# Row loads, normalisation, transposes and late modulation rows rearranged in an adaLN linear-attention and SwiGLU block

## The chip, the cores and the metric

The kernel runs on one core of a Trainium2 chip. A core has five engines, each with its own in-order instruction queue: TensorE (PE, with weight loads shown as PEld), VectorE (DVE), ScalarE (ACT), GpSimd (POOL) and SyncE (SP, which only issues transfers here). SP, ACT and POOL can issue DMAs. The metric is device microseconds of one execution; the times below are medians over several executions, and the profile is of one more.

## The reference

`x` is 2048 rows of 1024 (bf16). A conditioning vector `c` gives six modulation rows of 1024 through `w_mod`. With `H = 32` heads of width 32:

```python
mod = (_silu(c) @ w_mod).reshape(c.shape[0], 6, 1, -1)
sa, ca, ga, sb, cb, gb = ...
h = _layernorm(x, axis=-1) * (1 + ca) + sa
x = x + ga * _A_ref(h, A_wqkv, A_wo)          # linear attention
h = _layernorm(x, axis=-1) * (1 + cb) + sb
x = x + gb * _B_ref(h, B_w_gate, B_w_up, B_w_down)   # SwiGLU, F = 3584
# in _A_ref: q, k, v = split(x @ wqkv); phi(t) = where(t > 0, t + 1, exp(t)) + 1e-6
kv = einsum('bhsd,bhse->bhde', phi(k), v); z = einsum('bhsd->bhd', phi(k))
o = (phi(q) @ kv) / (phi(q) @ z + 1e-6); return o @ wo
```

## The kernel before

The 2048 rows are worked in four chunks of 512 (`sc` 0 to 3), each of four tiles of 128 rows (`st` 0 to 15; four a chunk). `M4` holds the normalised, transposed and modulated rows of a chunk as the matmul operand: 8 column blocks (`cc`) of 128 by 512.

The program is a list of labelled pieces of TensorE work in a hand-written order (`seq`), and a table of extra steps run after a piece (`put(label, step)`); nothing is reordered by a scheduler. The order is: the start with K of chunk 0, then V0 (eight groups), KV0 first half, Q0 first group, KV0 second half, the rest of Q0, K1, V1, KV1 first half, K2 first group, KV1 second half, the rest of K2, V2, and the same for K3 and V3, then Q1 to Q3 interleaved with the attention output, and the SwiGLU stage, which the change does not touch. Each group of K, V or Q is eight matmuls of 128x512 into one PSUM bank. `nextbank` hands out banks 0 to 4 in turn; a group that gets a bank must wait until its last user was read. Banks 5 to 7 hold the KV sums from KV0 on. K and Q groups are evacuated by `phi_to`: an exponential on ACT, then two operations on DVE. V groups are evacuated by one copy on ACT.

What the change touches:

- **Loads.** All loads go through the SP queue in program order: `c`, the row tiles (`load_x`, into six slots `xs`), the modulation weights of `ca` and `sa` in four steps (`load_wme`), K weights (`load_wk`), and V and Q weights (`load_cols`). Before, two row tiles come ahead of the first modulation step and two behind it.
- **Start.** `ln_a` takes mean and variance of a tile on DVE and `rstd` on POOL, `ln_nmr` the bias on DVE, `ln_xn_act` normalises on ACT. The four tiles of chunk 0 are transposed on TensorE (`tr0`) and copied to `M4` (`tr0_evac`, ACT for even tiles, DVE for odd). `mod_mm(p)` is 32 one-column matmuls into bank 7 that give two column blocks of `ca` and `sa`; `mod_apply(p)` copies them out and modulates these two blocks for all 512 rows. First K runs over the blocks for seven groups at once in banks 0 to 6, with `mod_mm(p + 1)` behind the tenth matmul of a step. `warm(n)` issues n matmuls on zeros.
- **Chunks 1 to 3.** `put_ln` places, two pieces apart, the statistics of a tile and the normalisation of the one before it (`ln_b`, on DVE), followed by `dma_start_transpose` on the ACT queue into `M4`. Then `modulate`, eight column blocks on DVE, in two steps.
- **Late modulation rows.** `ga`, `sb`, `cb`, `gb` (`LATE`): eight half rows, each loaded (`load_late`, 1 MB, three buffers) and multiplied (`late_mm`, 32 one-column matmuls), the two halves of a row into a bank from `nextbank` that is copied to `m1` by DVE after the second. `late_fin` makes `sbT`, `cb1T` or the spread copy `rep`; `late_bc` broadcasts `ga` or `gb` over the partitions by eight matmuls on `rep`. The multiplication of `wo` by `ga` is on DVE, in V2.

In the profile all buffers named `M...` show as `M`, PSUM banks as `bank`, and a line is that of the helper: L205 statistics, L211 `rstd`, L217 `nmr`, L223 and L228 normalise, L231 the transpose by DMA, L235 modulate, L248 to L250 `phi_to`, L253 K, L268 V, L276 Q, L285 KV, L316 and L319 a late piece and its copy, L327 `rep`, L334 broadcast, L341 transposes on TensorE, L379 `mod_mm`, L508, L514 and L533 the SwiGLU stage. L478 is the normalisation of the second layernorm, on POOL, L465 the attention output.

Of the kernel before, what the change touches and what calls it, by code (L numbers as in the profile page):

```python
# [21 lines left out]
def kernel(  # L22
# [13 lines left out]
    nc = tc.nc  # L36
# [114 lines left out]
    load_x(0)  # L151
    load_x(1)
    load_wme(0)
    load_x(2)
    load_x(3)
# [17 lines left out]
    mask = const.tile([P, KVW], BF16, name="mask")  # L173
    nc.gpsimd.memset(mask[:], 0.0)
    for j in range(HPC):
        rs = slice(j * DH, (j + 1) * DH)
        nc.gpsimd.memset(mask[rs, j * DH:(j + 1) * DH], 1.0)
        nc.gpsimd.memset(mask[rs, P + j:P + j + 1], 1.0)
    nc.gpsimd.memset(v_c[:, :, :, P:VW], 1.0)
# [21 lines left out]
    def ln_a(st):  # L201
# [10 lines left out]
        stat[st] = (mv, rstd)  # L212

    def ln_nmr(st):
        mv, rstd = stat[st]
# [5 lines left out]
    def ln_xn_act(st):  # L221
        rstd, nmr = stat.pop(st)
        nc.scalar.activation(out=xns[st % 6], in_=xs[st % 6], func=ACT.Identity, scale=rstd[:], bias=nmr[:])  # L223

    def ln_b(st):
        ln_nmr(st)
        rstd, nmr = stat.pop(st)
        nc.vector.tensor_scalar(out=xns[st % 6], in0=xs[st % 6], scalar1=rstd[:], scalar2=nmr[:],  # L228
                                op0=ALU.mult, op1=ALU.add)
        sc_, t = divmod(st, STC)  # L230
        nc.scalar.dma_start_transpose(out=M4[:, sc_, :, t * P:(t + 1) * P], in_=xns[st % 6])  # L231

    def modulate(sc_, cc, sT, c1T):
        h = M4[:, sc_, cc, :]
# [71 lines left out]
    late_acc = {}  # L306

    def late_mm(i):
        q, kb = LATE[i // 2][0], i % 2
        if kb == 0:  # L310
            late_acc[q] = nextbank()
        mps = late_acc[q]
        for ii in range(NB // P):
            col = kb * (NB // P) + ii
            for j in range(DC):
                nc.tensor.matmul(mps[:, col:col + 1], lhsT=wml[i % 3][:, j, ii * P:(ii + 1) * P],  # L316
                                 rhs=scT[:, j:j + 1], start=(j == 0), stop=(j == DC - 1))
# [32 lines left out]

    warm(14)
    ln_a(0)
    ln_a(1)
    ln_nmr(0)
    ln_xn_act(0)
    tr0(0)
    warm(2)
    ln_a(2)
    ln_nmr(1)
    ln_xn_act(1)  # L360
    tr0_evac(0)
    tr0(1)
    warm(2)
    ln_a(3)
    ln_nmr(2)
    ln_xn_act(2)
    tr0_evac(1)
    tr0(2)
    ln_nmr(3)
    ln_xn_act(3)  # L370

# [10 lines left out]
    def mod_apply(p):  # L382
# [5 lines left out]
        modulate(0, 2 * p, saT, ca1T)  # L388
# [304 lines left out]
```

## Time and profile before

| what | us |
|---|---|
| runs | 878.88, 883.75, 884.09 (median 883.75) |
| the profiled execution, whole | 880.06 |
| its span, first to last instruction | 878.3 |
| TensorE matmuls busy | 843.1 (96%) |
| VectorE busy | 331.5 (38%) |
| ScalarE busy | 144.1 (16%) |
| GpSimd busy | 58.9 (7%) |
| chain that ended last, TensorE's share | 88% |

The mean granted TensorE clock is 0.983. The three largest TensorE groups, L508, L514 and L533, are the SwiGLU stage, which begins near 249 us. A busy TensorE is not TensorE at its peak: a matmul of 512 columns counts as busy for 0.38 us on average while the next one already runs in its shadow, so prices are taken from the distance between starts. An idle time in the timeline stands in brackets behind the instruction that ends it, with the engine, tile and line whose end released it; where that engine had long been done, the release was another's.

### The profile page before, as it was taken

Reading aid. Unit: us, or ns where it says so; the run is one execution under the profiler, and the core shown is the slowest. Engines: PE = TensorE matmul, PEld = TensorE weight load, DVE = VectorE, ACT = ScalarE, POOL = GpSimd, SP = SyncE. Lnnn points to the kernel's source line nnn. Section 1 sums busy time; section 2 is a strip of 40 time slices with the busy share of each in tenths; the row PEclk is TensorE's granted clock in tenths of the full one; section 3 lists DMA queues with packets and bytes.
Section 4 is the critical chain, followed back from the end, with each engine's and each line's share of the span. In section 5 each row is a group of like instructions: output and inputs, shape, how many; then the busy total and the mean of one; then the engine's idle time right before and its main releaser. Section 6 shows DMA issues by size and latency. Waiting matters only on the chain.

```text
span 878.3 us, 10840 instructions
## 1 busy us (share of the span) xinstructions
PE 843.1 (96%) x4361; PEld 399.2 (45%) x4446; DVE 331.5 (38%) x643; ACT 144.1 (16%) x270; POOL 58.9 (7%) x114
## 2 busy tenths in 40 slices
PE   6989788899999999999999999999999999999998
PEld 3444343454444444444444444444444444444444
DVE  4557336629775565532121122121121221212212
ACT  4222222233231111111111000111100111100000
POOL 1010001001403222210000000000000000000000
PEclk6999889999999999999999999999999999999999
DMA  9984743404649889987788313555512455302220
GB/s 280 349 186 138 166 129 79 112 1 85 171 100 217 225 219 220 209 186 241 216 252 273 109 48 109 148 161 154 159 44 72 136 159 155 108 6 73 66 72 25
DMA packets 203764, 128.65 MB, mean 146 GB/s; under 512 B 50497, under 2 KB 189889, under 8 KB 203713
## 3 DMA queue, kind: packets, MB, share of 16 engines
q1 hardware_dynamic: 150336, 95.44, 37.2%
q10 hardware_dynamic: 51072, 24.12, 13.8%
q0 software_dynamic: 2304, 8.39, 2.5%
q8 instruction: 35, 0.57, 0.3%
q14 instruction: 17, 0.13, 0.1%
HBM read 103.81 MB, written 12.58 MB: 133 GB/s over the span
## 4 chain that ended last, share of the span: by engine, by line
PE 88%; DVE 5%; DMA 3%; issue 1%; ACTq 1%; ACT 1%; SPq 0%; POOL 0%; DVEq 0%
PE bank L514 22%; PE bank L533 22%; PE bank L508 22%; PE bank L465 6%; PE bank L276 6%; PE bank L253 5%; PE bank L268 2%; DMA M<-M 2%; DVE stats L205 1%; DVE M L250 1%; ACTq L231 1%; PE bank L438 1%; DMA M<-in_A_x_dram 1%; DVE e L249 1%; PE bank L285 1%
## 5 line engine op out<-in xcount | busy, mean ns | idle before, releaser
L514 PE MATMUL bank<-M,M 128*128 128x512 bf16 x881 | 210.4, 379 | 0.8
L508 PE MATMUL bank<-M,M 128*128 128x512 bf16 x871 | 209.7, 379 | 1.3
L516 DVE TENSOR_TENSOR M<-bank,e 128x512 bf16<-128x512 f32 x112 | 77.5, 692 | 275.1 <-PE bank L514 265.7
L533 PE MATMUL bank<-M,M 128*128 128x512 bf16 (+1 forms) x687 | 146.9, 370 | 0.6
L511 ACT ACTIVATE e<-bank 128x512 f32<-128x512 f32 x112 | 66.8, 597 | 439.7 <-PE bank L508 403.1
L533 PEld LDWEIGHTS <-M 128*128 128x128 bf16 x924 | 90.4, 98 | 103.3
L514 PEld LDWEIGHTS <-M 128*128 128x128 bf16 x896 | 87.7, 98 | 105.7
L508 PEld LDWEIGHTS <-M 128*128 128x128 bf16 x896 | 87.3, 98 | 103.9
L537 DVE TENSOR_TENSOR M<-bank,gb_bc 128x512 f32<-128x512 f32 (+1 forms) x33 | 22.3, 675 | 149.2 <-PE bank L533 135.3
L253 PE MATMUL bank<-M,M 128*128 128x512 bf16 x246 | 61.6, 396 | 9.8 <-DVE M L235 7.3
L268 PE MATMUL bank<-M,M 128*128 128x512 bf16 x247 | 58.1, 389 | 8.5 <-DVE m L319 5.2
L465 PE MATMUL bank<-M,M 128*128 128x512 bf16 x254 | 57.8, 379 | 0.1
L248 ACT ACTIVATE e<-bank 128x512 f32<-128x512 f32 x64 | 37.5, 598 | 118.5 <-PE bank L253 56.2
L276 PE MATMUL bank<-M,M 128*128 128x512 bf16 x250 | 56.6, 379 | 0.3
L533 PE MATMUL bank<-M 128*128 128x512 bf16 x219 | 50.7, 379 | 0.3
L249 DVE TENSOR_SCALAR e<-e 128x512 f32<-128x512 f32 x64 | 27.9, 436 | 50.5 <-ACT e L248 50.5
L250 DVE SCALAR_TENSOR_TENSOR M<-bank,e 128x512 bf16<-128x512 f32 x64 | 44.3, 692 | 3.6
L253 PEld LDWEIGHTS <-M 128*128 128x128 bf16 x256 | 24.7, 100 | 40.8 <-DVE M L235 12.5
L268 PEld LDWEIGHTS <-M 128*128 128x128 bf16 x256 | 25.3, 100 | 39.3 <-issue 11.6
L465 PEld LDWEIGHTS <-M 128*128 128x128 bf16 x256 | 24.9, 98 | 29.8
L276 PEld LDWEIGHTS <-M 128*128 128x128 bf16 x256 | 24.6, 98 | 27.9
L467 DVE TENSOR_TENSOR M<-bank,M 128x512 f32<-128x512 f32 x32 | 22.1, 690 | 14.4 <-PE bank L465 14.3
(66 smaller groups left out, 328.5 us busy)
## 6 DMA issues: line engine op xcount, KB each, us to landing
M<-in_B_w_gate_dram SPq DMA_DIRECT2D x56, 512.0 KB, 3.9
M<-in_B_w_up_dram SPq DMA_DIRECT2D x56, 512.0 KB, 5.1
M<-in_w_mod_dram SPq DMA_DIRECT2D x8, 1024.0 KB, 7.5
x_scratch<-M POOLq DMA_DIRECT2D x16, 512.0 KB, 5.8
M<-x_scratch ACTq DMA_DIRECT2D x16, 512.0 KB, 3.5
M<-in_B_w_down_dram SPq DMA_DIRECT2D x6, 1024.0 KB, 8.4
M<-in_A_x_dram SPq DMA_DIRECT2D x16, 256.0 KB, 7.6
M<-in_w_mod_dram SPq DMA_DIRECT2D x8, 512.0 KB, 7.0
```

The source lines that it names most:

```text
L248: nc.scalar.activation(out=e[:], in_=acc, func=ACT.Exp)
L249: nc.vector.tensor_scalar(out=e[:], in0=e[:], scalar1=1.0, scalar2=PHI_EPS, op0=ALU.min, op1=ALU.add)
L250: nc.vector.scalar_tensor_tensor(out=dst, in0=acc, scalar=0.0, in1=e[:], op0=ALU.max, op1=ALU.add)
L253: nc.tensor.matmul(acc[:], lhsT=M4[:, sc_, cc, t * P:(t + 1) * P], rhs=wk[:, cc, h * NB:(h + 1) * NB], start=(cc == 0), stop=(cc == DC - 1))
L268: nc.tensor.matmul(acc[:], lhsT=M4[:, sc_, cc, t * P:(t + 1) * P], rhs=wv[:, cc, h * NB:(h + 1) * NB], start=(cc == 0), stop=(cc == DC - 1))
L276: nc.tensor.matmul(acc[:], lhsT=wq[:, cc, qc * P:(qc + 1) * P], rhs=M4[:, sc_, cc, :], start=(cc == 0), stop=(cc == DC - 1))
L465: nc.tensor.matmul(acc[:], lhsT=oTs[st % 3][:, cc, :], rhs=wo[:, cc, hs], start=(cc == 0), stop=(cc == DC - 1))
L508: nc.tensor.matmul(g_ps[:], lhsT=wg_blk[:, cc, fs], rhs=M4[:, sc_, cc, :], start=(cc == 0), stop=(cc == DC - 1))
L511: nc.scalar.activation(out=sg[:], in_=g_ps[:], func=ACT.Silu)
L514: nc.tensor.matmul(u_ps[:], lhsT=wu_blk[:, cc, fs], rhs=M4[:, sc_, cc, :], start=(cc == 0), stop=(cc == DC - 1))
L516: nc.vector.tensor_tensor(out=gus[sc_][:, f, :], in0=u_ps[:], in1=sg[:], op=ALU.mult)
L533: nc.tensor.matmul(y_ps[:, 0:w], lhsT=gus[sc_][:, f, t * P:(t + 1) * P], rhs=wd(f)[:, c0:c1], start=(f == 0), stop=(f == FC - 1))
```

## The change

1. The four row tiles of chunk 0 are loaded ahead of the first modulation weights.
2. At the start the statistics of all four tiles come first; `nmr` moves from DVE to POOL; tile 2 is normalised on POOL, the other three on ACT; the masks and the ones of `v_c` are written on POOL behind that. First K begins tile by tile: the first two column blocks of tiles 0 and 1 are modulated and multiplied, then those of tiles 2 and 3, with the transposes of tile 3 and `mod_mm(1)` in between. Warm matmuls go from 14 + 2 + 2 to 21 + 3.
3. In chunks 1 to 3 `ln` takes statistics on DVE, `rstd`, `nmr` and the normalisation on POOL, and the transpose is issued on the SP queue. The labels are a little earlier.
4. The late rows accumulate in a free part of bank 7 (columns 320 and up), not in a bank from `nextbank`, and are spread over chunks 1 and 2 instead of chunk 1. The steps that use them, the load of `wo` and its multiplication by `ga` move back accordingly.

```diff
-    load_x(0)
-    load_x(1)
+    for st in range(STC):
+        load_x(st)
     load_wme(0)
-    load_x(2)
-    load_x(3)
     load_wk(0, 2)
...
         nmr = small.tile([P, 1], F32, name="nmr")
-        nc.vector.tensor_scalar(out=nmr[:], in0=mv[:, 0:1], scalar1=rstd[:], scalar2=-1.0,
+        nc.gpsimd.tensor_scalar(out=nmr[:], in0=mv[:, 0:1], scalar1=rstd[:], scalar2=-1.0,
                                 op0=ALU.mult, op1=ALU.mult)
...
+    def ln_xn(st, pool):
+        rstd, nmr = stat.pop(st)
+        if pool:
+            nc.gpsimd.tensor_scalar(out=xns[st % 6], in0=xs[st % 6], scalar1=rstd[:], scalar2=nmr[:],
+                                    op0=ALU.mult, op1=ALU.add)
+        else:
+            nc.scalar.activation(out=xns[st % 6], in_=xs[st % 6], func=ACT.Identity, scale=rstd[:], bias=nmr[:])
+
+    def ln(st):
+        ln_stats(st)
+        ln_xn(st, True)
         sc_, t = divmod(st, STC)
-        nc.scalar.dma_start_transpose(out=M4[:, sc_, :, t * P:(t + 1) * P], in_=xns[st % 6])
+        nc.sync.dma_start_transpose(out=M4[:, sc_, :, t * P:(t + 1) * P], in_=xns[st % 6])
...
-        if kb == 0:
-            late_acc[q] = nextbank()
-        mps = late_acc[q]
+        mps = bank[7][:, 320 + 8 * q:328 + 8 * q]
...
-                                 rhs=scT[:, j:j + 1], start=(j == 0), stop=(j == DC - 1))
+                                 rhs=scT[:, j:j + 1], start=False, stop=(j == DC - 1), skip_group_check=True)
...
+    warm(21)
+    for st in range(STC):
+        ln_stats(st)
+    ln_xn(2, True)
...
+    ln_xn(0, False)
+    tr0(0)
+    warm(3)
+    ln_xn(1, False)
+    tr0(1)
+    tr0_evac(0)
+    tr0_evac(1)
+    mod_mm(0)
+    mod_rows(0)
+    modulate(0, 0, saT, ca1T, 0, 2 * P)
+    modulate(0, 1, saT, ca1T, 0, 2 * P)
+    tr0(2)
+    ln_xn(3, False)
...
+    for g in (0, 1):
+        for cc in (0, 1):
+            kmm(bank[g], 0, G[g][0], G[g][1], cc)
     tr0(3)
     tr0_evac(3)
-    mod_apply(0)
...
+    for g in (2, 3):
+        for cc in (0, 1):
+            kmm(bank[g], 0, G[g][0], G[g][1], cc)
+    mod_mm(1)
+    mod_rows(1)
+    for g in (4, 5, 6):
+        for cc in (0, 1):
+            kmm(bank[g], 0, G[g][0], G[g][1], cc)
+    modulate(0, 2, saT, ca1T)
+    modulate(0, 3, saT, ca1T)
+    for p in (1, 2):
...
+    put_ln(1, [("V", 0, 1), ("V", 0, 2), ("V", 0, 3), ("V", 0, 4), ("Q", 0, 2), ("Q", 0, 3)])
     for sc in (2, 3):
...
+        put_ln(sc, [("K", sc - 1, 1), ("K", sc - 1, 3), ("K", sc - 1, 5), ("K", sc - 1, 7),
+                    ("V", sc - 1, 4), ("V", sc - 1, 6)])
-    put(("V", 0, 2), lambda: load_late(0), lambda: load_late(1), lambda: load_late(2))
+    put(("V", 0, 6), lambda: load_late(0), lambda: load_late(1), lambda: load_late(2))
...
-    lab = [("K", 1, i) for i in range(8)] + [("V", 1, i) for i in range(8)]
+    lab = [(k, sc, i) for sc in (1, 2) for k in ("K", "V") for i in (2, 6)]
...
+    put(("K", 1, 7), lambda: late_fin(2))
+    put(("V", 1, 1), lambda: late_bc(2, ga_bc))
+    put(("V", 1, 7), lambda: late_fin(3))
+    put(("K", 2, 0), lambda: nc.sync.dma_start(out=wo, in_=wo_v))
+    put(("K", 2, 7), lambda: late_fin(4))
+    put(("V", 2, 7), lambda: late_fin(5))
+    put(("K", 3, 1), lambda: late_bc(5, gb_bc))
     for cc in range(DC):
-        put(("V", 2, cc), lambda cc=cc: nc.vector.tensor_tensor(out=wo[:, cc, :], in0=wo[:, cc, :], in1=ga_bc[:],
+        put(("V", 3, cc), lambda cc=cc: nc.vector.tensor_tensor(out=wo[:, cc, :], in0=wo[:, cc, :], in1=ga_bc[:],
```

Three places show what moves. The lines of the changed kernel have other numbers. On ACT in V0 (CAST is the copy of a V group into `v_c`), before and now:

```order
L271 CAST M_81<-bank_73 128x4x128
L231 DMA_TRANSPOSE M_80<-M_83 128x8x128
L271 CAST M_81<-bank_74 128x4x128
L231 DMA_TRANSPOSE M_80<-M_83 128x8x128
L271 CAST M_81<-bank_70 128x4x128
```

```order
L260 CAST M_81<-bank_73 128x4x128
L260 CAST M_81<-bank_74 128x4x128
L260 CAST M_81<-bank_70 128x4x128
L260 CAST M_81<-bank_71 128x4x128
L260 CAST M_81<-bank_72 128x4x128
L237 ACTIVATE e<-bank_73 128x512
```

The transposes that stood between the copies are gone from ACT; the exponential of Q0 follows the last copy.

On DVE at the copy of a late row (`m`) and its spread copy `rep`, before in the middle of K1 and now at its end:

```order
L319 CAST m_131<-bank_73 128x8
L249 TENSOR_SCALAR e<-e 128x512
L250 SCALAR_TENSOR_TENSOR M_81<-bank_71,e 128x512
L205 BN_STATS stats<-M_83 128x6 x2
L207 BN_AGGR mv<-stats 128x2
L209 TENSOR_SCALAR veps<-mv 128x1
L217 TENSOR_SCALAR nmr<-mv,rstd 128x1
L228 TENSOR_SCALAR M_83<-M_83,rstd,nmr 128x1024
L327 COPY rep<-m_131 128x1024
```

```order
L304 CAST m_120<-bank_77 128x8
L238 TENSOR_SCALAR e<-e 128x512
L239 SCALAR_TENSOR_TENSOR M_81<-bank_73,e 128x512
L196 BN_STATS stats<-M_83 128x6 x2
L198 BN_AGGR mv<-stats 128x2
L200 TENSOR_SCALAR veps<-mv 128x1
L312 COPY rep<-m_120 128x1024
L224 TENSOR_SCALAR M_80<-M_80,ca1T,saT 128x512 x8
```

`nmr` and the normalisation have left DVE, the row is copied out of bank 7 instead of bank 3, and all eight modulations of chunk 2 follow `rep` directly.

On SP from the last weights of Q on, before and now:

```order
L148 DMA M_78<-in_A_wqkv_dram 128x8x512 x3
L304 DMA M_79<-in_w_mod_dram 128x8x512 x3
L137 DMA M_83<-in_A_x_dram 128x1024 x4
L304 DMA M_79<-in_w_mod_dram 128x8x512 x5
L607 DMA M_82<-in_A_wo_dram 128x8x1024
```

```order
L148 DMA M_78<-in_A_wqkv_dram 128x8x512 x3
L220 DMA_TRANSPOSE M_80<-M_83 128x8x128 x4
L293 DMA M_79<-in_w_mod_dram 128x8x512 x3
L137 DMA M_83<-in_A_x_dram 128x1024 x4
L220 DMA_TRANSPOSE M_80<-M_83 128x8x128
L293 DMA M_79<-in_w_mod_dram 128x8x512
L220 DMA_TRANSPOSE M_80<-M_83 128x8x128 x2
```

The four transposes of chunk 1 now stand between the weights of Q and the first late rows, and those of chunk 2 alternate with late loads.

More of the change, by code (lines that the diff above doesn't have):

```diff
@@ L172 @@
     nc.gpsimd.memset(den_eps_t[:], DEN_EPS)
[L173 to L179, printed above, removed]
     saT = const.tile([P, DC], BF16, name="saT")
@@ L590 @@
[L590 removed]
+        for t in range(STC):
+            put(labels[t], lambda t=t: ln(sc_ * STC + t))
+        for i in range(2):
+            put(labels[STC + i],
+                lambda i=i: [modulate(sc_, cc, saT, ca1T) for cc in range(4 * i, 4 * i + 4)])
+    put_ln(1, [("V", 0, 1), ("V", 0, 2), ("V", 0, 3), ("V", 0, 4), ("Q", 0, 2), ("Q", 0, 3)])
     for sc in (2, 3):
[L592 to L593 removed]
```

83 lines of the change are left out of this document (19 added, 64 removed).

## The prediction

> **What bounds the kernel now.** I read the page first (span, memory rate), then the TensorE timeline of the first 190 us, row by row, then what ACT, DVE and GpSimd do in each gap of it, then the landing times of transfers. The page:
>
> ```profile
> span 878.3 us, 10840 instructions
> ...
> GB/s 280 349 186 138 166 129 79 112 1 85 171 100 217 225 219 220 209 186 241 216 252 273 109 48 109 148 161 154 159 44 72 136 159 155 108 6 73 66 72 25
> ```
>
> A slice is 22 us. Transfers fill the first two (280 and 349 GB/s) and have room from then on. The change stands in the phases K, V and Q of the four row chunks, so the TensorE timeline there carries the rest (start us, duration, line, count, and in brackets the idle time ahead of it and who ended it):
>
> ```profile
> 16.83 1.01 PE L341 MATMUL bank<-ident,M 128*128 128x128 bf16 x8
> 19.43 0.61 PE L253 MATMUL bank<-M,M 128*128 128x512 bf16 x1 [1.58 <-DVE M L235]
> ...
> 31.84 6.08 PE L253 MATMUL bank<-M,M 128*128 128x512 bf16 x25
> 37.75 13.98 PE L268 MATMUL bank<-M,M 128*128 128x512 bf16 x63
> 51.56 1.07 PE L285 MATMUL bank<-M 128*128 128x129 bf16 x16
> 52.47 1.89 PE L276 MATMUL bank<-M,M 128*128 128x512 bf16 x8
> 54.20 0.28 PE L285 MATMUL bank<-M 128*128 128x129 bf16 x2
> ...
> 58.77 12.03 PE L276 MATMUL bank<-M,M 128*128 128x512 bf16 x54
> 70.64 3.62 PE L253 MATMUL bank<-M,M 128*128 128x512 bf16 x16
> 74.09 0.94 PE L316 MATMUL bank<-scT,M 128*128 128x1 bf16 x32
> 74.89 3.61 PE L253 MATMUL bank<-M,M 128*128 128x512 bf16 x15
> ...
> 88.35 1.89 PE L253 MATMUL bank<-M,M 128*128 128x512 bf16 x8 [1.89 <-DVE M L250]
> ...
> 96.22 0.59 PE L268 MATMUL bank<-M,M 128*128 128x512 bf16 x1 [5.20 <-DVE m L319]
> 97.02 5.05 PE L268 MATMUL bank<-M,M 128*128 128x512 bf16 x14 [0.22 <-issue]
> ...
> 115.48 1.07 PE L285 MATMUL bank<-M 128*128 128x129 bf16 x16
> 119.53 0.61 PE L253 MATMUL bank<-M,M 128*128 128x512 bf16 x1 [2.98 <-DVE M L235]
> ...
> 124.65 3.64 PE L253 MATMUL bank<-M,M 128*128 128x512 bf16 x16
> 128.13 0.61 PE L334 MATMUL bank<-ident,rep 128*128 128x128 bf16 x8
> ...
> 137.21 7.07 PE L268 MATMUL bank<-M,M 128*128 128x512 bf16 x31
> 146.28 3.61 PE L268 MATMUL bank<-M,M 128*128 128x512 bf16 x16 [2.01 <-DVE M L250]
> ...
> 154.03 1.07 PE L285 MATMUL bank<-M 128*128 128x129 bf16 x16
> 157.06 1.36 PE L253 MATMUL bank<-M,M 128*128 128x512 bf16 x4 [1.97 <-DVE M L235]
> ...
> 162.32 12.25 PE L253 MATMUL bank<-M,M 128*128 128x512 bf16 x55
> ```
>
> The undisturbed prices stand in it. V of chunk 0 is eight groups of eight matmuls from 37.75 to 51.56: 13.81, so 1.73 a group and 0.216 a matmul. Half of a KV step is 52.47 - 51.56 = 0.91. A piece of a late row (32 one-column matmuls) is 74.89 - 74.09 = 0.80. A broadcast is at most 0.61. TensorE is the bound: what it does not spend on these prices is what a schedule can win. From the end of Q0 on:
> - KV0's second half takes 54.20 to 58.77 = 4.57, due 0.91: 3.7 lost.
> - K1 and V1 with eight late pieces and one broadcast take 70.64 to 115.48 = 44.84, due 16 x 1.73 + 8 x 0.80 + 0.6 = 34.7: 10.1 lost. The brackets name it: a bank not yet evacuated (1.89), then 5.20 for the cast `m1` of a late row whose bank `nextbank` wants back.
> - KV1 with K2's first group, 115.48 to 124.65 = 9.17, due 2 x 0.91 + 1.73 = 3.55: 5.6 lost, begun by the wait for modulation (2.98).
> - V2, 137.21 to 154.03 = 16.82, due 13.81: 3.0 lost, begun by a late evacuation (2.01).
> - KV2 with K3's first group, 154.03 to 162.32 = 8.29, due 3.55: 4.7 lost, again modulation (1.97).
> Together 27.1. Part of it is no idle time but matmuls at a slow clock behind a gap (14 in 5.05 at 97.02, 0.36 each).
>
> **The start.** First K now begins at 19.43 and V0 at 37.75.
>
> ```profile
> 4.10 1.28 DVE L205 BATCH_NORM_STATS2 stats<-M 128x6 f32<-128x512 bf16 x2 [2.98 <-DMA M<-in_A_x_dram]
> ...
> 5.74 1.28 DVE L205 BATCH_NORM_STATS2 stats<-M 128x6 f32<-128x512 bf16 x2
> 5.91 0.56 POOL L211 TENSOR_TENSOR rstd<-veps,neg_half 128x1 f32<-128x1 f32 x1 [3.38 <-DVE veps L209]
> ...
> 9.89 1.29 DVE L205 BATCH_NORM_STATS2 stats<-M 128x6 f32<-128x512 bf16 x2 [2.32 <-DMA M<-in_A_x_dram]
> ```
> ```profile
> L476 POOL TENSOR_SCALAR nmr<-mv,rstd 128x1 f32<-128x1 f32 x16 | 4.8, 301 | 1.7
> ```
> ```profile
> 223.28 1.20 POOL L478 TENSOR_SCALAR M<-M,rstd,nmr 128x1024 bf16<-128x1024 f32 x1
> ```
>
> DVE needs 5.74 - 4.10 = 1.64 a tile and waits 2.32 for the third, which comes behind the first modulation weights. With all four tiles first, 1 MB is in at about the end of the second statistics, so DVE goes through: 4.10 + 4 x 1.64 = 10.7. Then GpSimd, in order: `rstd` 0.56, `nmr` 0.30 (now on GpSimd; the row is of the same form), normalising tile 2 at 1.20 (the nearest row has the same size with an f32 input): 12.7, with hand-overs 13.0. Eight transposes (1.01): TensorE starts first K at 14.0. The masks on GpSimd stand behind that and nothing needs them before KV0. The modulation weights of the first step come 0.5 MB later in the queue than before but, at 280 GB/s, 2.1 MB is in by 10, ahead of its use near 11.
>
> From 14.0 to V0: 64 matmuls at 0.216 = 13.8, three modulation pieces of 0.80 = 2.4, the last transposes 1.0, and some 1.2 for four hand-overs to DVE: 32.4. Saved 37.75 - 32.4 = 5.3. Cover: first K eats 1 MB of rows, 4.2 MB of modulation and 2.1 MB of K weights, 7.3 MB in all; the page's rates give 6.2 MB at 22 and the rest near 25.5, with about 1 us to complete 26.5; the last chunk is used near 27.6. So this cover is thin: 1 us. V weights and rows 4 to 7 follow the same queue and are wanted 5 us later than they land.
>
> **Transposes from ACT to SyncE.** In V0 the ACT queue now holds:
>
> ```profile
> 49.14 3.20 ACTq L231 DMA_TRANSPOSE M<-M  x1
> ...
> 52.46 3.28 ACTq L231 DMA_TRANSPOSE M<-M  x1
> ```
>
> ACT spends that time on issuing, and the copies of V behind it release KV0 late. On SyncE, twelve issues cost ACT nothing; KV0's 3.7 goes whole. What is queued behind a waiting transpose on SyncE: late weights, rows of the next chunk and `wo`. Chunk 1: DVE is done with K0's evacuations at about 42.7 - 5.3 = 37.4, GpSimd needs 0.56 + 0.30 + 1.20 with gaps 2.2 a tile, so tile 7 goes out at 37.4 + 1.64 + 4 x 2.2 = 47.8. Three late loads and four tiles behind it, 4.2 MB, are in near 62 at 349 GB/s with issue and completion; K1 begins at 32.4 + 13.8 + 2 x 0.91 + 13.8 = 61.8 and wants tile 8 two groups later at 65.3. Covered by 3.
>
> How long a transpose takes in SyncE's queue no row shows; on ACT's:
>
> ```profile
> DMA to landing us min/median/max: 3.0/5.2/14.2
> ```
>
> The 14.2 is the one beside `wo`; in one queue it follows the load instead of sharing with it, and `wo` now starts a chunk later. Deadlines from issue to landing: 11 us in chunk 1, about 8 in chunks 2 and 3 (tile 15 goes out near 24.5 after K2's start, the eight modulations must end at 32.7, they take 2.8, less overlap). I take 5.2, so the 5.6 and 4.7 go; I put back 0.5 for chunk 3. Ends: 0 and 9 for one chunk.
>
> **Normalise on GpSimd; late rows in bank 7.** DVE loses 0.55 + 0.20 and its waits for GpSimd per tile; late rows take no `nextbank` bank, so the 5.20 and 1.89 lose their cause. The pieces are the same eight; four move from K1/V1 to K2/V2, no change in the sum. What is late next is the broadcast of `ga`:
>
> ```profile
> 85.10 0.68 DVE L327 COPY rep<-m 128x1024 bf16<-128x1024 bf16 x1
> ```
> ```profile
> L248 ACT ACTIVATE e<-bank 128x512 f32<-128x512 f32 x64 | 37.5, 598 | 118.5 <-PE bank L253 56.2
> ...
> L250 DVE SCALAR_TENSOR_TENSOR M<-bank,e 128x512 bf16<-128x512 f32 x64 | 44.3, 692 | 3.6
> ```
> ```profile
> 222.35 0.43 DVE L249 TENSOR_SCALAR e<-e 128x512 f32<-128x512 f32 x1 [0.69 <-ACT e L248]
> ...
> 224.08 0.68 DVE L249 TENSOR_SCALAR e<-e 128x512 f32<-128x512 f32 x1 [0.57 <-ACT e L248]
> ```
>
> K1 ends on TensorE after 8 x 1.73 + 2 x 0.80 = 15.4, and the broadcast is due two groups later, at 18.9. DVE: exponential 0.60 + 0.2, then 0.43 + 0.69, statistics 1.64, `rep` 0.68: 15.4 + 4.3 = 19.7. TensorE waits 0.8. That is the low end. DVE's total in K1 is 8 x 1.12 + 4 x 1.64 = 15.5 against TensorE's 15.4, so it has no reserve, and GpSimd takes some: the L249 that began at 224.08, inside the normalise of 223.28 to 224.48, ended 0.28 after it and took 0.68 where the other took 0.43. An L249 that began with a normalise would wait 1.2. One in K1 caught early and one in part moves `rep` by 2: 2.8. I take 2. The Trainium skill (SBUF — State Buffer, Who interferes with whom) says that a DVE operation in a two-port mode and a GpSimd operation exclude each other for the whole instruction; the 0.68 row agrees, and by the page the whole 1.2 could be met at each normalise, which is the first rival.
>
> The multiplication of `wo` by `ga` moves to V3, where DVE has only that: hidden, eight at 0.68 in 13.8. It frees V2's evacuations, so the 3.0 goes.
>
> **Sum.** 5.3 + 27.1 = 32.4 off; 2.0 for `rep` and 0.5 for chunk 3 back: 29.9. The profiled execution took 880.06 for its span of 878.3, so 850.2 for one like it. The median of the runs shown, 883.75, is 3.7 above it and the lowest 1.2 below; I add 0.8 and say 851.
>
> **Rivals.**
> 1. GpSimd holds DVE in full: 0.56 + 0.30 + 1.20 = 2.1 at each of four tiles, 8.3 a chunk. Five banks give four groups less an evacuation, 6.9 - 1.9 = 5.0, so K itself waits some 3; `rep` would come 8 late, and tile 15 with it. 8 + 6 beyond what I have put back: 864. For it: the 0.68 row. Against: that row lost 0.25, and only L249 of the evacuations shows it.
> 2. Transposes land late: at 14.2 each, modulation misses K2's and K3's start by 3 and 6, each with a slow clock behind it (8 matmuls at 0.15 more, and half a KV step; 2.6), and K1's by 0 to 3. 15 back: 865. For it: SyncE's loads lie ahead of them. Against: the median.
> 3. First K runs slow: TensorE has gaps of 1 to 1.4 before 14.0. Its first 14 matmuls at 0.36 instead of 0.216 cost 2.0: 853, inside my range. Against: full speed behind the gaps at 88.35 (eight in 1.89). The Trainium skill (TensorE: Matmul & The Clock Gate, Part 1) has the clock fall after an idle window of about 3.4 us; the 2.98 gap with a slow clock behind it is shorter than that, the 5.20 one agrees.
> 4. Slower: the late rows wait for their weights. TensorE takes its instructions in order, and a late load stands behind waiting transposes on SyncE. Load i+3 is asked for behind piece i and used three pieces, twelve groups or 20.7 us, later; a transpose may hold it for the 5 us between two tiles. That leaves 16 for a load whose landing was
>
> ```profile
> DMA to landing us min/median/max: 5.5/7.5/11.7
> ```
>
> From 16 us on each further microsecond counts eight times; at 21 the gain is gone: (21 - 16) x 8 = 40 back, 890. Nothing shows such landings.
> 5. It does nothing: the gaps come back elsewhere, within 1% of before.
>
> **Chances.** My case 0.55 (846 to 857), first rival 0.17, second 0.12, third 0.08, slower 0.03, no effect 0.05. The range 845 to 865 takes in the first three rivals and leaves out the last two, and outliers of the others, 0.2 at most. A change of less than 1% (875 to 892) can't be told from none here. Faster 0.92, same 0.05, slower 0.03.
>
> **What would show it.** First K at 14 and V0 at 32 to 33, else the start is wrong. No idle time in KV0's second half. The broadcast of `ga` with a bracket of 0.8 to 2.8 naming `rep`. K2 and K3 beginning straight behind the half KV step: a bracket that names modulation, ended by a transpose, is the second rival. L249 with a mean near 0.45 is my case, above 0.8 the first rival. I'd be wrong altogether if V0 or K1 waited for tiles or weights: then SyncE's order is the new bound.

## The result and the profile after

The changed kernel takes 848.59 us (848.46 to 848.69), the kernel before, run beside it on the same chip, 881.32 (878.72 to 884.09): a ratio of 0.9628, interval 0.9588 to 0.9668. The predicted time was 851. From the page of the changed kernel, the span, the busy times, the transfer rate by slices and the chain that ended last:

```profile
span 846.8 us, 10977 instructions
...
PE 837.2 (99%) x4452; PEld 395.3 (47%) x4452; DVE 323.5 (38%) x617; ACT 143.9 (17%) x269; POOL 80.3 (9%) x143
...
GB/s 283 314 244 115 284 187 67 1 119 158 98 217 217 217 219 210 192 245 240 243 240 178 69 52 168 152 150 149 106 75 69 151 154 158 84 16 65 75 69 26
...
PE 95%; SPq 2%; DVE 1%; DMA 1%; issue 0%; ACT 0%; DVEq 0%
```

TensorE's share of the last chain went from 88% to 95%, and its mean granted clock from 0.983 to 1.00: fewer matmuls ran at a slow clock. The first two slices of the transfer rate, 283 and 314 (280 and 349 before), are not higher together; the start did not become faster by faster loads. The TensorE timeline of the changed kernel (L326 transposes, L242 K, L257 V, L265 Q, L274 KV, L343 the first modulation rows, L319 the broadcast):

```profile
13.15 0.62 PE L326 MATMUL bank<-ident,M 128*128 128x128 bf16 x8 [1.82 <-POOL M L211]
13.61 1.03 PE L242 MATMUL bank<-M,M 128*128 128x512 bf16 x4
...
21.36 0.55 PE L343 MATMUL bank<-scT,M 128*128 128x1 bf16 x16 [0.28 <-DMA M<-in_w_mod_dram]
...
26.32 0.55 PE L343 MATMUL bank<-scT,M 128*128 128x1 bf16 x16 [0.79 <-DMA M<-in_w_mod_dram]
...
32.65 13.98 PE L257 MATMUL bank<-M,M 128*128 128x512 bf16 x64
...
49.10 1.07 PE L274 MATMUL bank<-M 128*128 128x129 bf16 x16
50.01 12.25 PE L265 MATMUL bank<-M,M 128*128 128x512 bf16 x56
62.09 5.34 PE L242 MATMUL bank<-M,M 128*128 128x512 bf16 x24
...
82.11 0.62 PE L319 MATMUL bank<-ident,rep 128*128 128x128 bf16 x8 [0.99 <-DVE rep L312]
...
94.53 1.07 PE L274 MATMUL bank<-M 128*128 128x129 bf16 x16
...
98.07 3.62 PE L242 MATMUL bank<-M,M 128*128 128x512 bf16 x16
...
127.17 1.07 PE L274 MATMUL bank<-M 128*128 128x129 bf16 x16
...
130.71 1.89 PE L242 MATMUL bank<-M,M 128*128 128x512 bf16 x8
...
157.06 1.07 PE L274 MATMUL bank<-M 128*128 128x129 bf16 x16
```

The distances between starts give the account. KV3, the last row above, began in the kernel before at 188.22:

```profile
188.22 1.07 PE L285 MATMUL bank<-M 128*128 128x129 bf16 x16
```

It begins at 157.06 now, so 31.2 of the 31.5 by which the span fell lie ahead of it.

| stretch | before | after | less |
|---|---|---|---|
| up to V0 | 37.75 | 32.65 | 5.1 |
| KV0, second half (49.10 to 50.01) | 4.57 | 0.91 | 3.7 |
| K1 and V1 (62.09 to 94.53) | 44.84 | 32.44 | 12.4, of it 3.2 for four late pieces moved to K2 and V2 |
| KV1 and K2's first group (94.53 to 98.07) | 9.17 | 3.54 | 5.6 |
| the rest of K2, and V2 (98.07 to 127.17) | 29.38 | 29.10 | 0.3, with four late pieces (3.2) more |
| KV2 and K3's first group (127.17 to 130.71) | 8.29 | 3.54 | 4.7 |

From V0 to 300 us the timeline has one idle bracket, 0.99 for `rep`. So the time went where the prediction looked for it. Whether for its reasons is a question for the runs.

### The profile page after: what moved, and what is told of

It reads as the page before. It is cut to its first block, busy times and chain, and to the rows that moved or that the text cites. A ratio compares the mean times of both kernels' runs of the same rounds, so it can differ in the third digit from the quotient of the medians.

```text
span 846.8 us, 10977 instructions
## 1 busy us (share of the span) xinstructions
PE 837.2 (99%) x4452; PEld 395.3 (47%) x4452; DVE 323.5 (38%) x617; ACT 143.9 (17%) x269; POOL 80.3 (9%) x143
## 4 chain that ended last, share of the span: by engine, by line
PE 95%; SPq 2%; DVE 1%; DMA 1%; issue 0%; ACT 0%; DVEq 0%
PE bank L534 23%; PE bank L515 23%; PE bank L509 23%; PE bank L466 7%; PE bank L265 7%; PE bank L257 6%; PE bank L242 5%; DMA M<-in_w_mod_dram 1%; PE bank L439 1%; PE bank L274 1%; SPq L145 1%; SPq L142 1%; PE bank L301 1%; DVE stats L196 0%; DVE M L239 0%; DVE e L238 0%
## 5 line engine op out<-in xcount | busy, mean ns | idle before, releaser
L242 PE MATMUL bank<-M,M 128*128 128x512 bf16 x256 | 58.3, 379 | 0.4 <-DVE M L334 0.3
L265 PE MATMUL bank<-M,M 128*128 128x512 bf16 x256 | 57.5, 379 | 0.0
L257 PE MATMUL bank<-M,M 128*128 128x512 bf16 x256 | 56.7, 379 | 0.0
L238 DVE TENSOR_SCALAR e<-e 128x512 f32<-128x512 f32 x64 | 27.8, 434 | 41.3 <-ACT e L237 41.3
L257 PEld LDWEIGHTS <-M 128*128 128x128 bf16 x256 | 24.7, 98 | 29.0
L265 PEld LDWEIGHTS <-M 128*128 128x128 bf16 x256 | 24.6, 98 | 27.9
L242 PEld LDWEIGHTS <-M 128*128 128x128 bf16 x256 | 24.0, 97 | 28.1 <-DVE M L224 1.3
```

What stands on the lines that cost most here:

```text
L238: nc.vector.tensor_scalar(out=e[:], in0=e[:], scalar1=1.0, scalar2=PHI_EPS, op0=ALU.min, op1=ALU.add)
L242: nc.tensor.matmul(acc[:], lhsT=M4[:, sc_, cc, t * P:(t + 1) * P], rhs=wk[:, cc, h * NB:(h + 1) * NB], start=(cc == 0), stop=(cc == DC - 1))
L257: nc.tensor.matmul(acc[:], lhsT=M4[:, sc_, cc, t * P:(t + 1) * P], rhs=wv[:, cc, h * NB:(h + 1) * NB], start=(cc == 0), stop=(cc == DC - 1))
L265: nc.tensor.matmul(acc[:], lhsT=wq[:, cc, qc * P:(qc + 1) * P], rhs=M4[:, sc_, cc, :], start=(cc == 0), stop=(cc == DC - 1))
```

## The experiments

The theory under test is the prediction's list: the start, the transposes' queue, the late rows' banks and the normalisation each take away the stalls that it named. The rivals: one of them takes away more than its own, and another nothing. The kernels undo one part of the changed kernel (six), do one part alone (two) or two parts (one) on the kernel before, separate two readings of the queue (one), or try to go further (two).

### Transposes back on ACT's queue

```diff
-        nc.sync.dma_start_transpose(out=M4[:, sc_, :, t * P:(t + 1) * P], in_=xns[st % 6])
+        nc.scalar.dma_start_transpose(out=M4[:, sc_, :, t * P:(t + 1) * P], in_=xns[st % 6])
```

> The changed kernel with the twelve transposes of chunks 1 to 3 issued from the ACT queue again; the normalisation stays on GpSimd. Theory (the queue matters: ACT stands behind each transpose while it waits for GpSimd and issues, so V copies and exponentials come late): KV0's second half loses 2 to 9 again, K1/V1 some more; 855 to 861 us, and transposes land later than the 3.2 us median on SyncE. Rival (the gain came from taking normalisation off DVE, the queue is indifferent): 848.6 within 1, KV0's second half at 0.91.

It took 883.4 (882.99 to 884.94), a ratio of 1.0008 (0.9993 to 1.0022) to the kernel before. The expectation was far off: with this one line undone, the rest of the change gains nothing in sum. Its TensorE timeline has V0 at 32.25, so the start was kept, and then these waits:

```profile
91.32 3.57 PE L257 MATMUL bank<-M,M 128*128 128x512 bf16 x8 [3.90 <-DVE M L239]
...
103.11 1.03 PE L319 MATMUL bank<-ident,rep 128*128 128x128 bf16 x8 [8.22 <-DVE rep L312]
```

They name DVE, for an evacuated bank and for `rep`, and DVE was late because ACT was. ACT's timeline in K1 (ACTq is the instruction queue of ACT, where the transposes are issued):

```profile
79.64 1.25 ACTq L220 DMA_TRANSPOSE M<-M  x1
80.99 1.09 ACT L237 ACTIVATE e<-bank 128x512 f32<-128x512 f32 x2 [6.62 <-issue]
88.06 1.25 ACTq L220 DMA_TRANSPOSE M<-M  x1
89.41 1.09 ACT L237 ACTIVATE e<-bank 128x512 f32<-128x512 f32 x2 [7.33 <-issue]
```

Two exponentials run, then ACT idles 7.33 until the next transpose is out, 8.42 behind the last one. It is a loop. The transpose stands in ACT's in-order queue until the tile is normalised; the normalisation needs DVE's statistics; these stand on DVE behind the evacuations of two groups; and the evacuations need the two exponentials that stand on ACT behind the transpose before. Two groups are due every 3.46 and come every 8.42.

### Only the transposes' queue changed, on the kernel before

The same one line, in the other direction, on the kernel before.

> The kernel before with one part of the change: the transposes of chunks 1 to 3 issued from SyncE instead of ACT. Theory (ACT loses its issue times; on one queue wo comes behind the last transpose of chunk 2 instead of sharing with it): KV0's second half gains 3.7, the wait for modulation at K2 3 to 5.6; 873 us (871 to 877). Rival (loads stand behind transposes that wait for DVE, so late rows or row tiles come late): the gain is eaten, 880 or above.

It took 857.1 (854.33 to 858.33), ratio 0.9718 (0.9687 to 0.9749), well below the expected 871 to 877: 24.5 off, where 14.0 was the prediction's price for the queue (3.7, 5.6 and 4.7). The timeline of TensorE shows what came on top:

```profile
84.19 1.89 PE L253 MATMUL bank<-M,M 128*128 128x512 bf16 x8 [0.44 <-DVE M L250]
...
88.70 5.23 PE L268 MATMUL bank<-M,M 128*128 128x512 bf16 x16 [1.85 <-DVE m L319]
...
123.40 13.98 PE L268 MATMUL bank<-M,M 128*128 128x512 bf16 x64
```

V2 runs through without a loss, with the multiplication of `wo` still in it and the normalisation still on DVE. K1 and V1 take 39.41 (67.92 to 107.33): 5.4 of their 10.1 are gone, and the 1.89 for an evacuated bank has become 0.44. The trace of before holds the same loop. ACT in the kernel before, at the turn from K2 to V2:

```profile
136.44 1.26 ACTq L231 DMA_TRANSPOSE M<-M  x1
137.75 1.09 ACT L248 ACTIVATE e<-bank 128x512 f32<-128x512 f32 x2 [4.92 <-PE bank L253]
143.09 1.25 ACTq L231 DMA_TRANSPOSE M<-M  x1
144.38 0.60 ACT L248 ACTIVATE e<-bank 128x512 f32<-128x512 f32 x1 [5.55 <-PE bank L268]
```

and DVE of the same kernel:

```profile
142.51 0.55 DVE L228 TENSOR_SCALAR M<-M,rstd,nmr 128x1024 bf16<-128x1024 bf16 x1
...
145.54 0.69 DVE L250 SCALAR_TENSOR_TENSOR M<-bank,e 128x512 bf16<-128x512 f32 x1
```

The bracket before 144.38 says that the exponential waited for TensorE's bank, but K2's last group had ended at 137.21, where V2 starts. What it waited for was the transpose in front of it, issued when the normalisation of 142.51 was done. The evacuation at 145.54 then released the bank that V2 got at 146.28. The period, 143.09 - 136.44 = 6.65, is the same loop as above. It is shorter because DVE itself normalises, in 0.55, the tile before the one whose statistics it has just taken; in the run above `rstd`, `nmr` and the normalisation on GpSimd ran from 85.82 to 88.03. With the transposes on SyncE the exponentials of K2 come one group apart (1.73).

### Transposes on ACT, but issued later

Is it the standing on ACT, or is it how long a transpose takes to land on that queue? On the kernel before, the transposes stay on ACT and go out one or two steps behind their normalisation:

```diff
+    def ln_t(st):
         sc_, t = divmod(st, STC)
         nc.scalar.dma_start_transpose(out=M4[:, sc_, :, t * P:(t + 1) * P], in_=xns[st % 6])
...
+        tl = [("V", 0, 5), ("V", 0, 6), ("V", 0, 7), ("V", 0, 7)] if sc_ == 1 else [
+            ("K", sc_ - 1, 6), ("V", sc_ - 1, 0), ("V", sc_ - 1, 2), ("V", sc_ - 1, 3)]
+        for t in range(STC):
+            put(tl[t], lambda t=t: ln_t(s0 + t))
```

> The kernel before with one edit: the transposes stay on ACT's queue, but each is issued one or two steps after its normalisation (the last of a chunk one group of matmuls later), so that ACT hardly ever stands behind a transpose that waits for its input. If that standing is what the change of queue removed (theory), most of the 24.5 comes off and ACT's exponentials stay about one group apart: 861 (857 to 865), a little above the 857.1 of the SyncE queue, since ACT still issues for 1.25 each and the transposes go out later. If the queue matters by how long a transpose takes to land beside SyncE's loads (rival), the landings stay at 5.2 in the median and 14 at most, the waits for modulation ahead of K2 and K3 stay (5.6 and 4.7), and only the delays of the other stages go: 870 or more.

It took 868.06 (867.45 to 871.2), ratio 0.9843 (0.9812 to 0.9873), between the two: each reading holds for its own stretches. The trace is of the slowest execution, 871.2. TensorE:

```profile
107.76 1.07 PE L287 MATMUL bank<-M 128*128 128x129 bf16 x16
114.45 3.59 PE L255 MATMUL bank<-M,M 128*128 128x512 bf16 x8 [5.62 <-DVE M L237]
...
132.17 13.98 PE L270 MATMUL bank<-M,M 128*128 128x512 bf16 x64
...
148.42 1.36 PE L255 MATMUL bank<-M,M 128*128 128x512 bf16 x4 [1.36 <-DVE M L237]
```

KV0 loses nothing (the halves of KV and Q0's first group stand 0.91, 1.72 and 0.91 apart), V2 loses nothing (132.17 to 145.99), K1 and V1 take 39.37 like the run on SyncE. In K1, V1 and V2, 5.47 + 3.00 = 8.5 were thus ACT standing behind a transpose that waited for its input. KV0's 3.66 has another cause, the issuing itself. In the kernel before, the second transpose in V0 had its input ready at 49.11:

```profile
48.56 0.55 DVE L228 TENSOR_SCALAR M<-M,rstd,nmr 128x1024 bf16<-128x1024 bf16 x1
```

ACT began to issue it at 49.14 and took 3.20, and 3.28 for the third, whose input was ready at 51.44. All four stood ahead of the last copy of V, at 57.18. In this run two of the four stand behind that copy, which comes at 53.65.

The waits for modulation ahead of K2 and K3 are still there, 8.3 and 4.1 lost. ACT and SP of this run in V1, and DVE's modulation:

```profile
98.78 9.15 ACTq L233 DMA_TRANSPOSE M<-M  x1
```
```profile
95.76 0.65 SPq L613 DMA_DIRECT2D M<-in_A_wo_dram  x1
```
```profile
113.98 1.38 DVE L237 TENSOR_SCALAR M<-M,ca1T,saT 128x512 bf16<-128x512 bf16 x4 [14.38 <-DMA M<-M]
```

The tile had been normalised by 92.31, ACT issued the transpose from 98.78, took 9.15 over it, beside `wo`, and the modulation began 6 later. On SyncE's queue the same transpose was issued at 95.33, ahead of `wo` at 97.57, and the modulation began at 102.20. Chunk 3 gives the fairer comparison, since both runs issue its last transpose at the same place, 9.2 behind the start of V2, with the tile just normalised: the modulation begins 6.6 behind the issue on ACT (141.37 to 147.95) and 3.5 behind the issue on SyncE (132.6 to 136.11). So the prediction's order is there: in one queue the loads stand behind the transposes rather than beside them. That this order is what makes the landing short is argued, not shown.

The Trainium skill (DMA: Bandwidth & Descriptors, Rules for kernel authors) says that spreading DMAs over SP, ACT and GpSimd gives no bandwidth and saves only issue time. No run here compares the bandwidth, and the issue on ACT did not save time: it grew from 1.25 to 9.15.

The 8.3 is more than the 5.6 of before, though `wo` went out just ahead of the last transpose of chunk 2 there too (103.48 and 104.78). K1 and V1 end 7.7 earlier here (107.76 for 115.48), but the modulation begins only 5.1 earlier (113.98 for 119.06).

### Only the late rows' bank, on the kernel before

```diff
-        if kb == 0:
-            late_acc[q] = nextbank()
-        mps = late_acc[q]
+        mps = bank[7][:, 320 + 8 * q:328 + 8 * q]
...
```

> The kernel before with one part of the change: the late rows accumulate in bank 7 instead of a bank from nextbank. Theory (the 5.20 and 1.89 and the slow clock behind them come from the held bank): K1 and V1 together get 5 to 8 shorter, 875 us. Rival (DVE was late anyway and the wait comes back as a wait for an evacuated bank or for rep): 0 to 2 shorter, 880.

875.62 (875.51 to 876.46), ratio 0.9934 (0.9911 to 0.9956). The time is as expected; K1 and V1, from 44.84 to 40.49, fall by 4.35, less than the expected 5 to 8. The wait of 1.89 for an evacuated bank is gone. A row of the TensorE timeline shows what stays of the 5.20, a late piece that waits for the copy of the row before it:

```profile
95.21 0.94 PE L312 MATMUL bank<-scT,M 128*128 128x1 bf16 x32 [3.45 <-DVE m L315]
```

A row's place in bank 7 is its own, yet the next piece waits until DVE has copied the row before it, and DVE is late by the loop.

### Queue and bank together, on the kernel before

Both edits above.

> The kernel before with two edits: the twelve DMA transposes on SyncE's queue, and the late rows in bank 7. The queue alone gave 857.1, the bank alone took 6.0 off. If ACT waiting behind a transpose and the late rows' banks are separate causes, the 6.0 come off in full: 851.1. My theory is that they overlap, since part of what the bank freed was time in which evacuations were late behind a transpose: of K1 and V1 4.7 is left in the run with the queue alone, of which the bracket that names the copy of a late row (1.85) and the slow matmuls behind it (about 1.5) go, and a wait for the broadcast's spread copy stays: 853.8 (852.5 to 855).

854.51 (852.54 to 855.0), ratio 0.9677 (0.9645 to 0.9709), in the theory's range by the median, 2.6 under the queue alone. But the theory's reason, an overlap, is not in the timeline: K1 and V1 fall from 39.41 to 35.20, by 4.2, as they fell by 4.35 with the bank alone, and the spans differ by 856.5 - 852.6 = 3.9 here and 878.3 - 874.1 = 4.2 there. The medians (2.6 and 6.0) are less to be trusted here: the runs of the two kernels with the new queue lie 2.5 and 4 apart among themselves. The two causes are separate. By distances on TensorE the queue takes away 27.1 - 4.7 = 22.4 of the losses and the bank 4.2; with the 5.1 of the start that makes 31.7, against 31.5 by which the span fell.

### Late rows back in banks from `nextbank`

The reverse of the bank edit, in the changed kernel.

> The changed kernel with each late row in a bank from nextbank again, still spread over chunks 1 and 2. Theory (a held bank blocks the fifth group behind it until DVE has copied m, which stands behind DVE's other work): a wait for m of 1 to 3 us at the row of K1, 0.5 to 1 at the others; 852 us (850 to 855). Rival (the spread alone removed the wait): 848.6 within 0.5.

858.77 (858.35 to 858.84): 10.2 more, above the range. TensorE in K1 and K2:

```profile
78.68 3.57 PE L242 MATMUL bank<-M,M 128*128 128x512 bf16 x8 [2.83 <-DVE m L308]
...
118.15 2.95 PE L242 MATMUL bank<-M,M 128*128 128x512 bf16 x8 [2.83 <-DVE m L308]
```

The first fence row stands in K1, the second in K2. The waits for `m` (with two of 0.33 and 0.26 in V1 and V2) are 6.25; the rest is the slow clock behind them, eight matmuls in 3.57 and 2.95 where 1.89 is undisturbed, less the wait for `rep`, which is gone. The cause was right and its size not.

### Normalisation back on DVE; all late rows in chunk 1

Two more reversals, each alone. The first puts the normalisation of chunks 1 to 3 on DVE, a step behind the statistics; the second gives the late rows their old places.

```diff
-        ln_xn(st, True)
+        nc.vector.tensor_scalar(out=xns[st % 6], in0=xs[st % 6], scalar1=rstd[:], scalar2=nmr[:],
+                                op0=ALU.mult, op1=ALU.add)
...
```

> The changed kernel with the normalisation of chunks 1 to 3 on DVE again (a tile behind its statistics, as before), nmr on GpSimd and transposes on SyncE. Theory (DVE has no reserve in K1, three normalisations of 0.55 to 0.6 stand ahead of rep): the wait for rep grows from 0.99 to 2.8, all else as it is; 850.4 us (849.5 to 852). Rival (GpSimd holds DVE's port for about what DVE saves): 848.6 within 0.5, and the wait for rep stays near 1.

849.88 (849.21 to 851.75), 1.3 more, in the expected range, with a wait for `rep` below the expected 2.8; its row of the broadcast:

```profile
83.26 0.62 PE L320 MATMUL bank<-ident,rep 128*128 128x128 bf16 x8 [2.15 <-DVE rep L313]
```

That is 1.16 longer than the changed kernel's 0.99, and all that normalising on GpSimd is worth in chunks 1 to 3.

```diff
-    lab = [(k, sc, i) for sc in (1, 2) for k in ("K", "V") for i in (2, 6)]
+    lab = [("K", 1, i) for i in range(8)] + [("V", 1, i) for i in range(8)]
...
```

> The changed kernel with the late rows in bank 7 but all eight pieces, their broadcasts and the load of wo at the places of the kernel before, in chunk 1. Theory (the bank mattered; the spread only gives the weights time, which now come behind transposes on SyncE): 849.6 us (848 to 853), with short waits of a late piece for its weights. Rival (the spread is what removed the waits): 4 us or more slower, with waits at DVE's work and not at weights.

851.25 (851.02 to 852.14), 2.7 more, inside the range. Two late pieces wait for their weights, one of them for 0.35, the other for 2.41:

```profile
85.65 0.98 PE L301 MATMUL bank<-scT,M 128*128 128x1 bf16 x32 [2.41 <-DMA M<-in_w_mod_dram]
```

That is the mechanism of the fourth rival, a late load standing on SyncE behind transposes. With four groups between pieces, rather than two, the changed kernel has no such wait.

### The start: old load order; first K in one piece

```diff
-    for st in range(STC):
-        load_x(st)
+    load_x(0)
+    load_x(1)
     load_wme(0)
+    load_x(2)
+    load_x(3)
```

> The changed kernel with the old load order (two row tiles, first modulation weights, two row tiles). The third tile's statistics wait for its rows until 9.9 us as before and first K begins 2.4 later. Theory (the start now ends on transfers: the modulation weights of step 3 landed 0.79 late and those of step 2 0.28 late, and these do not move): 1.07 of the 2.4 is absorbed, V0 begins 1.3 later; 849.9 us. Rival (the chain of statistics and normalisation sets the start): V0 begins 2.4 later, 851.

851.65 (851.19 to 851.83), 3.1 more, outside both expectations. TensorE's timeline, and the windows of 4 us (columns: PE busy and count, then the other engines, then granted clock, transfer share, GB/s):

```profile
15.43 1.03 PE L328 MATMUL bank<-ident,M 128*128 128x128 bf16 x8 [4.35 <-POOL M L213]
```
```profile
16.00:20.00 4.00, 4.00 (x20) 2.12 (x18) 0.83 (x2) 2.29 (x2) 0.47 (x5) 0.50 1.17 309
```

The gap before tile 2 grows to 4.35 and TensorE comes back at half the clock. V0 starts at 35.51, 2.86 later. No modulation weight was waited for. By distances, tile 2 comes 2.28 later, the stretch from there to the second modulation piece takes 1.95 more, at half the clock, and the rest 1.37 less. So the theory's absorption is there, and the slow clock, which neither expectation had, used it up.

The second edit begins first K only behind the last transpose, for all four tiles at once:

```diff
-    modulate(0, 0, saT, ca1T, 0, 2 * P)
-    modulate(0, 1, saT, ca1T, 0, 2 * P)
...
+    modulate(0, 0, saT, ca1T)
+    modulate(0, 1, saT, ca1T)
+    for p in (0, 1, 2):
```

> The changed kernel with the first K begun only when all four tiles are transposed and modulated, with the loads and the order of statistics as changed. First K begins near 16.2 instead of 13.6, and by the tenth matmul is 1.7 behind. Theory (transfers end the start): 0.6 later in all, 849.2 us, the waits for modulation weights gone. Rival (compute ends it): 1.7 later, 850.3.

850.71 (850.55 to 850.88), 2.1 more, nearer the rival's 850.3 than the theory's 849.2; V0 at 34.84.

```profile
15.80 4.44 PE L242 MATMUL bank<-M,M 128*128 128x512 bf16 x10 [1.31 <-DVE M L224]
```

First K begins 2.19 later, and V0 as much. In between lie 19.04 in both kernels, of different things: here ten matmuls at 0.42 each (4.24 between starts) where 0.216 is full speed, 2.1 lost, in the changed kernel the transposes of tile 3 and 1.4 of waits. A start by tiles thus fills a gap with work; that it keeps the clock up is not shown, as the next run tells. The two reversals, 2.86 and 2.19, add up to 5.05, the start's 5.1. Since both hold matmuls at a slow clock, the agreement is no proof that they are separate parts.

### Two ways on

The broadcast of `ga` two groups later, so that `rep` is ready:

```diff
-    put(("V", 1, 1), lambda: late_bc(2, ga_bc))
+    put(("V", 1, 3), lambda: late_bc(2, ga_bc))
```

> The changed kernel with the broadcast of ga two V groups later (behind the fourth group of V1 instead of the second). Theory (the 0.99 wait is DVE reaching rep late, nothing more): the wait goes whole, 847.6 us. Rival (it turns into a wait for a bank further on): 848.6.

847.73 (846.97 to 847.92), as expected; its ratio to before is 0.9610 (0.9587 to 0.9634). The wait for `rep` is gone. Its start is that of the changed kernel, line for line, and yet it ran at another clock. Tile 2's transposes come behind a gap of 1.69, where the changed kernel had 1.82, and the granted clock from 12 to 16 us is 0.63, where the changed kernel had 1.00 (the columns are those above):

```profile
13.60 1.91 PE L242 MATMUL bank<-M,M 128*128 128x512 bf16 x4
```
```profile
12.00:16.00 4.00, 3.13 (x19) 2.04 (x20) 1.14 (x2) 3.05 (x3) 1.77 (x11) 0.63 1.16 316
```

These four matmuls take 1.70 between starts, 0.43 each. V0 begins at 32.89 all the same, only 0.2 later than in the changed kernel, since of its waits for modulation weights one of 0.18 is left. The run with the late rows in banks from `nextbank` has that start and that clock too, and V0 at 32.58. So the same start can run slow or not, and in these runs the waits for weights took up most of the difference.

With the later broadcast, tile 2 normalised on ACT and tile 3 on GpSimd:

```diff
-    ln_xn(2, True)
+    ln_xn(3, True)
...
     tr0_evac(0)
+    ln_xn(2, False)
...
-    ln_xn(3, False)
```

> As the run with the later broadcast, and at the start tile 2 is normalised on ACT and tile 3 on GpSimd. Tile 2's transposes come at 12.1 instead of 13.15, so first K could begin 0.4 to 1 earlier. Theory (transfers end the start): the wait for the last modulation weights grows by the same and V0 does not move, 847.6 us. Rival (the chain over GpSimd's normalisation sets the start): V0 0.4 to 1 earlier, 846.6 to 847.2.

847.66 (847.18 to 847.87), the same. First K begins at 12.21, 1.4 earlier than in the changed kernel, and V0 at 32.44, 0.2 earlier. The first of two brackets shows where the rest went:

```profile
21.16 0.55 PE L343 MATMUL bank<-scT,M 128*128 128x1 bf16 x16 [1.34 <-DMA M<-in_w_mod_dram]
```

TensorE overtakes the modulation weights. The start now ends with the transfers, not with the normalisation. Both kernels are 0.9 under the changed one, whose runs were all above theirs; the intervals of the ratios to before overlap, so that the gain rests on the bracket that is gone.

## Why the prediction came out right, and where its reasons did not

**The sum** was 29.9 off; the profiled execution took 848.62 against 880.06, so 31.4. Of the 1.5 between them 1.0 is `rep` and 0.5 the reserve for chunk 3, which was not needed. The stretches and their losses, read from distances on TensorE, all came back as predicted, and that is why the total is close: the prediction counted what TensorE did not spend on undisturbed prices. Two of its attributions failed. As the change makes all the edits at once, it did not matter to the total which edit a loss belonged to; that is luck.

**Start: right.** First K at 13.61 (predicted 14.0), V0 at 32.65 (32.4). The cover called thin was used up: the waits of 0.28 and 0.79 name the modulation weights. The third rival's slow clock did not come in the trace of the changed kernel. It came in the two runs that undid a part of the start, but also in two that left the start as it is. So neither the order of the loads nor the start by tiles is shown to keep it away; that it stayed away is in part luck, worth at most 0.2 at V0.

**KV0's 3.7: right.** ACT's 3.20 and 3.28 were spent on issuing, as the prediction says, with their inputs ready. It is in K1 to V2 that ACT stood for an input. With two of the four transposes behind the last copy of V, transposes on ACT cost KV0 nothing.

**K1 and V1's 10.1: the step "late rows take no `nextbank` bank, so the 5.20 and 1.89 lose their cause" failed in half.** The bank was worth 4.2; 5.4 was the loop of ACT and DVE, which the prediction did not have. Both stalls had both causes: with the bank alone the 1.89 went and 3.45 stayed where 5.20 had been, with the queue alone 0.44 and 1.85 stayed. The rest, 0.55, is the wait for `rep`.

**KV1's 5.6 and KV2's 4.7: right.** With ACT's standing removed and its queue kept, these waits stayed; on SyncE they went. No page of before showed a transpose's landing there; it is shorter and steadier than the 5.2 taken and the 14.2 feared. For L220, the transposes of the changed kernel:

```profile
DMA to landing us min/median/max: 3.1/3.2/6.7
```

The modulation of chunk 2 ended 1.9 ahead of its use, so the second rival had little room to spare. The fourth rival's sum is loose: at eight for each microsecond from 16 on, the gain of 29.9 would be gone near 19.7, not at 21.

**V2's 3.0: the step "it frees V2's evacuations" failed.** With the multiplication by `ga` left in V2 and the normalisation left on DVE, V2 lost nothing once the transposes were on SyncE. The prediction had the rows of ACT in V0 and read there that copies stand behind transposes; it didn't look at ACT in K1 to V2, where the brackets named DVE.

So the queue carries 22.4 by distances and 24.5 by medians, not 14.0, and undone it takes 34.8, more than the whole change gained. One reason shows in the rows: with the normalisation on GpSimd the loop is longer, 8.42 for 6.65.

**Put back: `rep` 0.99, for 2.0 taken and a low end of 0.8.** I had added for GpSimd holding DVE (first rival). The page's group of L238 and the normalisations on GpSimd (the line's durations, minimum, median and maximum in ns):

```profile
L238 DVE TENSOR_SCALAR e<-e 128x512 f32<-128x512 f32 x64 | 27.8, 434 | 41.3 <-ACT e L237 41.3
```
```profile
L211 POOL TENSOR_SCALAR M<-M,rstd,nmr x13: 1192/1249/1461, 11.8 to 116.8; 128x1024 bf16<-128x1024 bf16 x13
```

L238 kept the 0.43 of before, and it was GpSimd's instruction that grew, from 1.19 to 1.46. In K1 an L238 begins inside a normalisation:

```profile
70.50 1.46 POOL L211 TENSOR_SCALAR M<-M,rstd,nmr 128x1024 bf16<-128x1024 bf16 x1
```
```profile
70.63 0.43 DVE L238 TENSOR_SCALAR e<-e 128x512 f32<-128x512 f32 x1 [0.21 <-ACT e L237]
```

Of the stages that the change touches, only at the start was DVE held, beside the normalisation of tile 2 that ran from 11.84 to 13.09. DVE there and alone:

```profile
11.84 1.33 DVE L224 TENSOR_SCALAR M<-M,ca1T,saT 128x256 bf16<-128x256 bf16 x2
...
15.91 0.60 DVE L224 TENSOR_SCALAR M<-M,ca1T,saT 128x256 bf16<-128x256 bf16 x2
```

0.73 more for the two of them. The exclusion of the Trainium skill (SBUF — State Buffer, Who interferes with whom), on which that rival leaned, agrees with the start. In K1 to V2 no whole instruction of DVE was held; what delay there was fell on GpSimd, which had time.

**Open.** Why a transpose on ACT's queue issues and lands so slowly beside SyncE's loads is shown only as durations; no run looked at the packets. In the run with later transposes the trace is of an execution 3 above the others, so its waits at KV1 and KV2 may be larger than theirs. Of the start, the statistics taken first, `nmr` and tile 2 on GpSimd and the longer warm-up were not tried apart.

## What to carry to other kernels

An instruction that waits for its input in the queue of an engine that also evacuates holds everything behind it: before a DMA is issued from ACT, ask who produces its input, and whether that producer waits for ACT. Where brackets name an evacuation that is late, look at what stands in front of it on its own engine, since the bracket shows a release that may be long past. To know what each part of a change is worth, undo it and also do it alone: the bank was worth about 4 on the old kernel and 10 when taken out of the new one.

## What the runs showed of the hardware that was not expected

- A transpose's landing changed with its queue: in the kernel before 5.2 in the median and 14.2 at most, on ACT's queue; with nothing but the queue changed 3.4 and 6.7. Its issue on ACT took 1.25 to 3.28 in the kernel before, and 9.15 once, beside `wo`, in the run with later transposes; on SyncE, with nothing else changed, 1.23 to 2.19.
- The clock falls behind short gaps, and not always. With the same start, it stayed at 1.00 behind a gap of 1.82 in the changed kernel and fell to 0.63 (over 12 to 16 us) behind 1.69 in the run with the later broadcast; slow matmuls also came behind 2.83. The Trainium skill (TensorE: Matmul & The Clock Gate, Part 1) speaks of an idle window of about 3.4 us; a single gap of that length was not needed here.
- GpSimd and DVE delay each other in either direction: GpSimd's normalisation took up to 1.46 instead of 1.19 where DVE was busy, DVE's two modulations 1.33 instead of 0.60 in the one place where both began together. In the last run DVE began there 0.12 earlier (11.63 and 11.75), kept its 0.60, and GpSimd took 1.38.
